# Start of an FNet and gMLP kernel: x's first tiles from three queues, row 0 normed by VectorE, row 3's statistics by ScalarE

## The chip, the cores and the metric

The kernel runs on one core of a Trainium2 chip. The metric is the device time of one execution in microseconds (us). The engines are called TensorE (PE, with its weight loads PEld), VectorE (DVE), ScalarE (ACT), GpSimd (POOL) and SyncE (SP). SP, ScalarE and POOL can each issue DMAs; an instruction waits in the queue of its engine until those ahead of it have gone.

## The reference

All in float32, for one batch of S = 2048 rows and D = 512 columns:

```python
sa, ca, ga, sb, cb, gb = split(silu(c) @ w_mod, 6)
h = layernorm(x) * (1 + ca) + sa
a, b = h @ dft_hid_re.T, h @ dft_hid_im.T
x = x + ga * (dft_seq_re @ a - dft_seq_im @ b)        # FNet
h = layernorm(x) * (1 + cb) + sb
z = gelu(h @ w_in); z1, z2 = z[:, :896], layernorm(z[:, 896:])
x = x + gb * ((z1 * (w_sp @ z2 + b_sp)) @ w_out)      # gMLP
```

## The kernel before

A float32 product is made of three products of float32r parts: each operand is split into a high part (`hi`, by a copy that rounds) and a low part (`lo`, by a subtraction), and `matmul3` adds hi x hi, hi x lo and lo x hi.

The first stage is the product of the sequence matrices with the normed rows of x. It goes in 128 steps of 12 matmuls of 512 columns (`mm_a`). A step n takes one row tile s of x (128 rows) and one slice of a matrix block. For the first 32 steps (the first 512 output columns) blocks of `dft_seq_re` and `dft_seq_im` alternate every four steps, and row tiles 0 to 3 serve steps 0 to 7, tiles 4 to 7 the next eight, and so on. Steps 0 to 3 have an order of their own, line by line of operands: hi x hi for four column blocks, then the two mixed products.

What a step needs is prepared by these pieces:

- `load_x(g, ks, engs)` loads row tiles ks of group g in four DMAs, one for 32 partitions each, and goes through the queues of `engs` in turn. `load_block` loads a matrix block of 512 x 512 in four DMAs (or half of each row of it, s0 to s1); `load(b)` does so for block b into one of two `stage` buffers, by SP.
- `turn_one` and `turn_two` transpose one or two slices of a block on VectorE (lines 173 and 211). `prep_hi(n)` makes the high part `ah` (ScalarE, line 224; for step 0 VectorE, line 222) and `prep_lo(n)` the low part `al` (VectorE, line 230).
- `stats_first(s)` takes mean and variance of row tile s on VectorE (lines 348, 350), adds epsilon (351), takes the power -0.5 on POOL (352) and forms -mean x rstd on POOL (353). `norm_x(s)` norms the tile on ScalarE (line 119) into `xn`. `hi_h(s)` makes its high part `hh` on ScalarE (line 390), `lo_h(s)` its low part `hl` on VectorE (line 395). Column 0 of `xn` is set to 1 by POOL.
- `sum_x(s)` and `square_x(s)` are the other way to the statistics, used for row tiles from 10 on: ScalarE copies the tile and sums it (line 360), POOL scales the sum (361); ScalarE squares and sums (365), and POOL scales, takes the power and multiplies (366 to 368).
- `keep_busy(n, k)` gives TensorE n products of ones (line 311) whose result nobody reads, while the first loads are under way.
- `load_columns(j)` loads a block of `w_mod`; `weigh_column` transposes and weighs a slice of it on VectorE (lines 173 and 295), `sum_column` sums it on ScalarE (line 300), `scale_columns` finishes. `load_ht(j)` loads the hidden matrix into the buffer that the block of `w_mod` with j = 1 had.

The order of work on each engine is the order in which the program writes it (`manual_schedule`). Before step 0 it is written out by hand. From step 0 on, `prep(n)` puts `prep_lo(n + 2)`, the transpose for n + 4, and `prep_hi(n + 3)` ahead of step n, and `run(n)` calls what `at(n, ...)` has put down for that step, after its products. `al` has three buffers and `ah` four, so the preparation can be two to three steps ahead.

Of the kernel before, what the change touches and what calls it, by code (L numbers as in the profile page):

```python
# [8 lines left out]
F32 = mybir.dt.float32  # L9
F32R = mybir.dt.float32r  # L10
AF = mybir.ActivationFunctionType
ALU = mybir.AluOpType

P = 128
# [5 lines left out]
def fnet_gmlp_kernel(  # L20
# [32 lines left out]
    nc = tc.nc  # L53
    S, D = x.shape[1:]
# [11 lines left out]
    def pool(name, side="left", bufs=1):  # L66
        return tc.tile_pool(name=name, bufs=bufs, side=side, reuse_waits="tile")
# [11 lines left out]
    def bank(k, name):  # L79
        return psum.tile([P, 512], F32, tag=f"bank{k}", bufs=1, name=name)  # L80
# [37 lines left out]
    def apply(dst, src, scale_shift):  # L118
        nc.scalar.activation(dst, src, AF.Identity, bias=scale_shift[1], scale=scale_shift[0])
# [3 lines left out]
    def at(n, f, *a):  # L123
        fill.setdefault(n, []).append((f, a))
# [23 lines left out]
    def load_block(tile_, a, s0=0, s1=P, engs=(nc.sync,)):  # L148
        v = a.rearrange("(b j) (a s) -> a j b s", j=32, a=4)
        for q in range(4):  # L150
            engs[q % len(engs)].dma_start(tile_[32 * q:32 * q + 32, :, s0:s1], v[q][:, :, s0:s1])
# [20 lines left out]
    def squares(dst, block, k):  # L172
        nc.vector.transpose(dst.rearrange("p (b i) -> p b i", i=32), block[:, :, 32 * k:32 * k + 32])
# [13 lines left out]
    def slot(n):  # L187
        if n % 2 == 0:
            t = blocks.tile([P, 2, Q], F32, tag="t", bufs=2, name=f"t{n}")
            T[n], T[n + 1] = t[:, 0, :], t[:, 1, :]  # L190
        return T[n]

    def turn_one(n):
        squares(slot(n), stage[n // 4], n % 4)
# [22 lines left out]
    def prep_hi(n, eng=None):  # L217
        if n >= NE:
            return
        AH[n] = blocks.tile([P, Q], F32R, tag="ah", bufs=4, name=f"ah{n}")  # L220
        if eng:
            eng.tensor_scalar(AH[n], T[n], 1.0, None, op0=ALU.mult)
        else:
            nc.scalar.activation(AH[n], T[n], AF.Copy)  # L224

    def prep_lo(n):
        if n >= NE:
            return
        AL[n] = blocks.tile([P, Q], F32R, tag="al", bufs=3, name=f"al{n}")
        nc.vector.tensor_tensor(AL[n], T.pop(n), AH[n].bitcast(F32), op=ALU.subtract)  # L230
# [6 lines left out]
    spool = s1.enter_context(pool("spool", "right"))  # L237
# [5 lines left out]

    ccol = cpool.tile([P, ND], F32, name="ccol")
    ones = cpool.tile([P, P], F32, name="ones")
    nc.gpsimd.memset(ones, 1.0)
    mhalf = cpool.tile([P, 1], F32, name="mhalf")
    nc.gpsimd.memset(mhalf, -0.5)
    sc = cpool.tile([P, ND], F32, name="sc")
    busy = rows.tile([P, D], F32, tag="row", bufs=6, name="busy")  # L250
    nc.vector.memset(busy, 1.0)
# [55 lines left out]
    def keep_busy(n, k):  # L307

        ps = bank(k, "busyp")
        for _ in range(n):  # L310
            nc.tensor.matmul(ps, ones, busy, start=True, stop=True)
# [14 lines left out]
    X, XG, LN, NRM, h_hi, h_lo = {}, {}, {}, {}, {}, {}  # L326

    def load_x(g, ks=range(4), engs=(nc.sync,)):

        if g not in XG:  # L330
            if g % 2:
                XG[g] = spool.tile([P, 4, D], F32, tag="x", bufs=1, name=f"x{g}")
            else:
                XG[g] = hpool.tile([P, 4, D], F32, tag="h12", bufs=1, name=f"x{g}")
        k0, k1 = ks[0], ks[-1] + 1
        v = x.rearrange("(g a k i) d -> g a i k d", g=NQ, a=4, i=32)
        for a in range(4):
            engs[a % len(engs)].dma_start(XG[g][32 * a:32 * a + 32, k0:k1, :], v[g, a][:, k0:k1, :])
        for k in ks:
            X[4 * g + k] = XG[g][:, k, :]  # L340
# [1 line left out]
    def stats_x(s):  # L342
        NRM[s] = norm([X[s]], "x")

    def stats_first(s):

        m = spool.tile([P, 12], F32, tag="first", bufs=4, name=f"first{s}")
        nc.vector.bn_stats(m[:, :6], X[s])
        mv = m[:, 8:]
        nc.vector.bn_aggr(mv[:, :2], m[:, :6])  # L350
        nc.vector.tensor_scalar(mv[:, 1:2], mv[:, 1:2], EPS, None, op0=ALU.add)
        nc.gpsimd.tensor_tensor(mv[:, 2:3], mv[:, 1:2], mhalf, op=ALU.pow)
        nc.gpsimd.tensor_scalar(mv[:, 3:4], mv[:, 0:1], mv[:, 2:3], -1.0, op0=ALU.mult, op1=ALU.mult)
        NRM[s] = mv[:, 2:3], mv[:, 3:4]

    def sum_x(s):

        LN[s] = spool.tile([P, D], F32, tag="xn", bufs=4, name=f"xn{s}")
        m = NRM[s] = spool.tile([P, 4], F32, tag="sums", bufs=3, name=f"sums{s}")
        nc.scalar.activation(LN[s], X[s], AF.Copy, accum_out=m[:, 0:1])  # L360
        nc.gpsimd.tensor_scalar(m[:, 0:1], m[:, 0:1], -1.0 / D, 1.0, op0=ALU.mult, op1=ALU.mult)

    def square_x(s):
        m = NRM[s]
        nc.scalar.activation(LN[s], X[s], AF.Square, bias=m[:, 0:1], accum_out=m[:, 1:2])
        nc.gpsimd.tensor_scalar(m[:, 1:2], m[:, 1:2], 1.0 / D, EPS, op0=ALU.mult, op1=ALU.add)
        nc.gpsimd.tensor_tensor(m[:, 2:3], m[:, 1:2], mhalf, op=ALU.pow)
        nc.gpsimd.tensor_tensor(m[:, 3:4], m[:, 0:1], m[:, 2:3], op=ALU.mult)
        NRM[s] = m[:, 2:3], m[:, 3:4]

    def norm_x(s):

        if s not in LN:
            LN[s] = spool.tile([P, D], F32, tag="xn", bufs=4, name=f"xn{s}")
        if s > 3:
            nc.gpsimd.memset(LN[s][:, 0:1], 1.0)
        apply(LN[s][:, 1:], X.pop(s)[:, 1:], NRM.pop(s))

    def parts_h(s, t):

        return t[s].rearrange("p k (a i) -> p k a i", i=32), LN[s].rearrange("p (a k i) -> p k a i", a=4, i=32)

    def hi_h(s):
        if s < 12:
            h_hi[s] = hpool.tile([P, ND, P], F32R, name=f"hh{s}")
        else:
            if s == 12:
                h_hi["last"] = hpool.tile([P, 4, ND, P], F32R, tag="h12", bufs=1, name="hh12")
            h_hi[s] = h_hi["last"][:, s - 12]
        nc.scalar.activation(*parts_h(s, h_hi), AF.Copy)  # L390

    def lo_h(s):
        h_lo[s] = hpool.tile([P, ND, P], F32R, name=f"hl{s}")
        lo, h = parts_h(s, h_lo)
        nc.vector.tensor_tensor(lo, h, parts_h(s, h_hi)[0].bitcast(F32), op=ALU.subtract)
        LN.pop(s)
# [375 lines left out]


    both = (nc.sync, nc.scalar)
    load_x(0, range(1), both)
    stage[0] = blocks.tile([P, 16, P], F32, tag="stage", bufs=2, name="stage0")
    load_block(stage[0], src[0], 0, P // 2, both)
    load_x(0, range(1, 2), both)
    nc.scalar.activation(sc, ones[:, :ND], AF.Silu)
    load_x(0, range(2, 4))  # L780
    load_block(stage[0], src[0], P // 2, P)
    load(1)
    load_x(1, range(2))
    keep_busy(4, 5)
    for s in range(4):
        LN[s] = spool.tile([P, D], F32, tag="xn", bufs=4, name=f"xn{s}")
        nc.gpsimd.memset(LN[s][:, 0:1], 1.0)
    stats_first(0)
    norm_x(0)
    hi_h(0)  # L790
    turn_one(0)
    prep_hi(0, nc.vector)
    stats_first(1)
    lo_h(0)
    prep_lo(0)
    norm_x(1)
    hi_h(1)
    turn_one(1)
    prep_hi(1)
    stats_first(2)  # L800
    prep_lo(1)
    lo_h(1)
    norm_x(2)
    hi_h(2)
    turn_one(2)
    prep_hi(2)
    stats_first(3)
    turn_one(3)
    prep_hi(3)
    norm_x(3)  # L810
# [7 lines left out]
    at(2, load_row)  # L818
    at(9, silu_row)
    at(4, load_x, 2)  # L820
    at(5, load_columns, 1)
    at(8, load_x, 3)
    at(12, load_columns, 0)
    at(19, load_ht, 0)
    at(28, load_ht, 1)
    for s, n in ((4, 4), (5, 4), (6, 6), (7, 6), (8, 10), (9, 10)):
        m = n + (s == 9)
# [4 lines left out]
    for s, n in zip(range(10, NS), (11, 12, 15, 16, 18, 19)):  # L832
# [2 lines left out]
        at(n + 2, norm_x, s)  # L835
        at(n + 3, hi_h, s)
        at(n + 4, lo_h, s)
    for j, ns in ((1, (12, 14, 17, 18)), (0, (21, 22, 23, 24))):
        for k, n in enumerate(ns):
            at(n, weigh_column, j, k)  # L840
            at(n + 1, sum_column, j, k)
    at(20, scale_columns)

    def change_pools():
        s1.close()
# [225 lines left out]
```

## Time and profile before

| | |
|---|---|
| median of 3 runs | 956.17 us (956.03 to 956.31) |
| profiled execution | 957.03 us |
| its span, first to last instruction | 955.2 us |
| TensorE busy | 948.1 us (99%) |
| VectorE, ScalarE, POOL busy | 674.7, 367.1, 169.0 us |
| granted TensorE clock | 1.000 |

The profile lists for each engine when an instruction started, how long it took, and what ended the idle time before it. A number in the prediction like L395 is the line of the kernel, `hl<-xn,hh` are the tiles written and read, and x4 counts merged instructions.

### The profile page before, as it was taken

How to read it: one execution, taken by the hardware profiler on the slowest of the kernel's cores; microseconds unless marked ns; L12 is line 12 of the kernel's file. 1: busy time of each engine (PE TensorE's matmuls, PEld its weight loads, DVE VectorE, ACT ScalarE, POOL GpSimd, SP SyncE). 2: the span in 40 equal slices, each digit the busy share in tenths (PEclk: the TensorE clock that was granted, in tenths of full speed). 3: DMA queues.
4: the chain of work that ended last, by engine and by line, in shares of the span. 5: the costliest groups of instructions: out<-in, count | busy, mean ns of one | idle time of the engine just before them, and what ended most of it. 6: DMA issues, size and time to landing. Idle time of an engine off the chain costs nothing.

```text
span 955.2 us, 12247 instructions
## 1 busy us (share of the span) xinstructions
PE 948.1 (99%) x4196; PEld 788.1 (83%) x4196; DVE 674.7 (71%) x995; ACT 367.1 (38%) x630; POOL 169.0 (18%) x328
## 2 busy tenths in 40 slices
PE   8999999999999999999999999999999999999998
PEld 5878888888888888888888999888888888888886
DVE  6799857775575757765445577877778688885882
ACT  4585424232232212331444356634544343331221
POOL 2421000221621235114313344200000000000000
PEclk9999999999999999999999999999999999999999
DMA  9997553576538975995499854555545355833541
GB/s 208 218 217 153 116 137 90 148 180 154 143 78 212 276 216 147 273 265 154 154 287 302 308 183 155 145 135 132 138 114 120 90 132 133 209 92 121 192 164 60
DMA packets 249679, 161.27 MB, mean 169 GB/s; under 512 B 130192, under 2 KB 218512, under 8 KB 249488
## 3 DMA queue, kind: packets, MB, share of 16 engines
q1 hardware_dynamic: 236800, 122.59, 53.3%
q0 software_dynamic: 11424, 37.24, 10.6%
q10 hardware_dynamic: 1392, 0.66, 0.3%
q8 instruction: 33, 0.54, 0.3%
q14 instruction: 30, 0.25, 0.1%
HBM read 123.73 MB, written 36.70 MB: 168 GB/s over the span
## 4 chain that ended last, share of the span: by engine, by line
PE 98%; DVE 1%; DMA 0%; ACT 0%; issue 0%; POOL 0%; ACTq 0%; DVEq 0%
PE gp L96 12%; PE gp L97 12%; PE gp L95 12%; PE gw L97 10%; PE gw L95 10%; PE gw L96 9%; PE yp L95 3%; PE yp L97 3%; PE yp L96 3%; PE z2p L95 3%; PE z2p L96 3%; PE z2p L97 3%; PE op L97 3%; PE op L96 3%; PE z1p L97 3%; PE z1p L95 3%
## 5 line engine op out<-in xcount | busy, mean ns | idle before, releaser
L224 ACT ACTIVATE ah<-t 128x512 fp32r<-128x512 f32 x271 | 169.7, 627 | 345.8 <-PE gp L97 183.9
L230 DVE TENSOR_TENSOR al<-t,ah 128x512 fp32r<-128x512 f32 x272 | 185.7, 686 | 165.2 <-PE gp L96 63.7
L96 PE MATMUL gp<-al,hh 128*128 128x512 f32 x496 | 193.1, 389 | 0.6 <-DVE al L230 0.6
L95 PE MATMUL gp<-ah,hh 128*128 128x512 f32 x496 | 193.0, 389 | 0.0
L97 PE MATMUL gp<-ah,hl 128*128 128x512 f32 x496 | 192.9, 389 | 0.0
L97 PE MATMUL gw<-ah,bl 128*128 128x512 f32 x400 | 155.6, 389 | 0.0
L96 PE MATMUL gw<-al,bh 128*128 128x512 f32 x400 | 155.6, 389 | 0.0
L95 PE MATMUL gw<-ah,bh 128*128 128x512 f32 x400 | 155.6, 389 | 0.0
L96 PEld LDWEIGHTS gp<-al,hh 128*128 128x128 f32 x496 | 93.1, 188 | 20.2 <-DVE al L230 1.0
L95 PEld LDWEIGHTS gp<-ah,hh 128*128 128x128 f32 x496 | 93.1, 188 | 19.4
L97 PEld LDWEIGHTS gp<-ah,hl 128*128 128x128 f32 x496 | 93.1, 188 | 19.3
L211 DVE STREAM_TRANSPOSE t<-stage 128x1024 f32<-128x1024 f32 x70 | 86.7, 1239 | 7.8 <-DMA stage<-in_A_dft_seq_re_dram 6.6
L97 PEld LDWEIGHTS gw<-ah,bl 128*128 128x128 f32 x400 | 75.1, 188 | 15.7
L96 PEld LDWEIGHTS gw<-al,bh 128*128 128x128 f32 x400 | 75.1, 188 | 15.7
L95 PEld LDWEIGHTS gw<-ah,bh 128*128 128x128 f32 x400 | 75.1, 188 | 15.4
L205 DVE STREAM_TRANSPOSE t<-stage 128x1024 f32<-128x1024 f32 x56 | 69.4, 1239 | 0.8 <-DMA stage<-in_B_w_sp_dram 0.8
L617 POOL DMA_DIRECT2D s_d<-sj x64 | 35.2, 551 | 125.0 <-DVE sj L609 88.8
L639 ACT ACTIVATE bh<-z 128x512 fp32r<-128x512 f32 (+1 forms) x56 | 32.8, 586 | 61.8 <-PE gw L96 61.8
L95 PE MATMUL yp<-hth,gh 128*128 128x512 f32 x128 | 49.8, 389 | 0.0
L96 PE MATMUL yp<-htl,gh 128*128 128x512 f32 x128 | 49.8, 389 | 0.0
L97 PE MATMUL yp<-hth,gl 128*128 128x512 f32 x128 | 49.8, 389 | 0.0
L96 PE MATMUL z2p<-wil,ah 128*128 128x448 f32 x128 | 46.7, 365 | 0.0
(155 smaller groups left out, 1362.1 us busy)
## 6 DMA issues: line engine op xcount, KB each, us to landing
stage<-in_A_dft_seq_im_dram SPq DMA_DIRECT2D x64, 256.0 KB, 5.4
sj<-in_B_w_sp_dram SPq DMA_DIRECT2D x32, 512.0 KB, 7.7
s_d<-sj POOLq DMA_DIRECT2D x64, 256.0 KB, 4.5
stage<-s_d SPq DMA_DIRECT2D x128, 128.0 KB, 2.9
stage<-in_A_dft_seq_re_dram SPq DMA_DIRECT2D x60, 256.0 KB, 5.3
stage<-in_B_w_sp_dram SPq DMA_DIRECT2D x96, 128.0 KB, 3.0
stage<-h_d SPq DMA_DIRECT2D x32, 256.0 KB, 5.3
z_d<-z POOLq DMA_DIRECT2D x28, 256.0 KB, 6.6
```

Source lines behind the costliest of these rows:

```text
L95: nc.tensor.matmul(acc, ah, bh, start=first, stop=False, skip_group_check=go_on)
L96: nc.tensor.matmul(acc, ah, bl, start=False, stop=False, skip_group_check=go_on)
L97: nc.tensor.matmul(acc, al, bh, start=False, stop=last, skip_group_check=go_on)
L205: nc.vector.transpose(t.rearrange("p r (b i) -> p r b i", i=32), st[:, :, :, 16 * k:16 * k + 32])
L211: nc.vector.transpose(t.rearrange("p k (b i) -> p k b i", i=32), st[:, :, 32 * k:32 * k + 64].rearrange("p b (k i) -> p k b i", k=2))
L224: nc.scalar.activation(AH[n], T[n], AF.Copy)
L230: nc.vector.tensor_tensor(AL[n], T.pop(n), AH[n].bitcast(F32), op=ALU.subtract)
L617: nc.gpsimd.dma_start(s_d[m, r, g][b * P:(b + 1) * P, :], a)
L639: nc.scalar.activation(BH[p, k][:, :w], b_of(p, k), AF.Copy)
```

## The change

Loads: row tile 0 of x goes by SP, ScalarE and twice POOL, tile 1 by SP, POOL, ScalarE and POOL, tiles 2 and 3 by POOL alone. Before, SP and ScalarE shared tiles 0 and 1, and SP loaded tiles 2 and 3. The memset of `ones` moves from POOL to VectorE; POOL's other memsets come after its loads.

Row statistics: tile 0 is normed by VectorE itself (subtract the mean, times rstd). For tiles 1 and 2 VectorE instead of POOL forms -mean x rstd. Tile 3 takes its statistics by `sum_x` and `square_x`; `sum_x(3)` stands right after `hi_h(0)`, `square_x(3)` ahead of `stats_first(2)`. The order of `lo_h`, `prep_lo`, `norm_x` and `hi_h` of the first tiles is changed.

One idle product is left out (3 instead of 4). The load of `w_mod`'s columns 1 moves from step 5 to step 6, behind the load of block 4; their weighing from steps 12, 14, 17, 18 to 15, 17, 18, 20; `scale_columns` from 20 to 22; the load of the first hidden matrix from 19 to 21.

```diff
--- before.py
+++ after.py
@@ -243,9 +243,8 @@
 
     ccol = cpool.tile([P, ND], F32, name="ccol")
     ones = cpool.tile([P, P], F32, name="ones")
-    nc.gpsimd.memset(ones, 1.0)
+    nc.vector.memset(ones, 1.0)
     mhalf = cpool.tile([P, 1], F32, name="mhalf")
-    nc.gpsimd.memset(mhalf, -0.5)
     sc = cpool.tile([P, ND], F32, name="sc")
     busy = rows.tile([P, D], F32, tag="row", bufs=6, name="busy")
     nc.vector.memset(busy, 1.0)
@@ -342,7 +341,7 @@
     def stats_x(s):
         NRM[s] = norm([X[s]], "x")
 
-    def stats_first(s):
+    def stats_first(s, fold=True):
 
         m = spool.tile([P, 12], F32, tag="first", bufs=4, name=f"first{s}")
         nc.vector.bn_stats(m[:, :6], X[s])
@@ -350,8 +349,12 @@
         nc.vector.bn_aggr(mv[:, :2], m[:, :6])
         nc.vector.tensor_scalar(mv[:, 1:2], mv[:, 1:2], EPS, None, op0=ALU.add)
         nc.gpsimd.tensor_tensor(mv[:, 2:3], mv[:, 1:2], mhalf, op=ALU.pow)
-        nc.gpsimd.tensor_scalar(mv[:, 3:4], mv[:, 0:1], mv[:, 2:3], -1.0, op0=ALU.mult, op1=ALU.mult)
         NRM[s] = mv[:, 2:3], mv[:, 3:4]
+        if fold:
+            nc.vector.tensor_scalar(mv[:, 3:4], mv[:, 0:1], mv[:, 2:3], -1.0, op0=ALU.mult, op1=ALU.mult)
+        else:
+            nc.vector.tensor_scalar(LN[s][:, 1:], X.pop(s)[:, 1:], mv[:, 0:1], mv[:, 2:3],
+                                    op0=ALU.subtract, op1=ALU.mult)
 
     def sum_x(s):
 
@@ -372,7 +375,7 @@
 
         if s not in LN:
             LN[s] = spool.tile([P, D], F32, tag="xn", bufs=4, name=f"xn{s}")
-        if s > 3:
+        if s > 2:
             nc.gpsimd.memset(LN[s][:, 0:1], 1.0)
         apply(LN[s][:, 1:], X.pop(s)[:, 1:], NRM.pop(s))
 
@@ -772,39 +775,40 @@
 
 
     both = (nc.sync, nc.scalar)
-    load_x(0, range(1), both)
+    load_x(0, range(1), (nc.sync, nc.scalar, nc.gpsimd, nc.gpsimd))
     stage[0] = blocks.tile([P, 16, P], F32, tag="stage", bufs=2, name="stage0")
     load_block(stage[0], src[0], 0, P // 2, both)
-    load_x(0, range(1, 2), both)
+    load_x(0, range(1, 2), (nc.sync, nc.gpsimd, nc.scalar, nc.gpsimd))
+    load_x(0, range(2, 4), (nc.gpsimd,))
+    for s in range(3):
+        LN[s] = spool.tile([P, D], F32, tag="xn", bufs=4, name=f"xn{s}")
+        nc.gpsimd.memset(LN[s][:, 0:1], 1.0)
+    nc.gpsimd.memset(mhalf, -0.5)
     nc.scalar.activation(sc, ones[:, :ND], AF.Silu)
-    load_x(0, range(2, 4))
     load_block(stage[0], src[0], P // 2, P)
     load(1)
     load_x(1, range(2))
-    keep_busy(4, 5)
-    for s in range(4):
-        LN[s] = spool.tile([P, D], F32, tag="xn", bufs=4, name=f"xn{s}")
-        nc.gpsimd.memset(LN[s][:, 0:1], 1.0)
-    stats_first(0)
-    norm_x(0)
+    keep_busy(3, 5)
+    stats_first(0, False)
     hi_h(0)
+    sum_x(3)
     turn_one(0)
     prep_hi(0, nc.vector)
     stats_first(1)
+    norm_x(1)
+    hi_h(1)
     lo_h(0)
     prep_lo(0)
-    norm_x(1)
-    hi_h(1)
     turn_one(1)
     prep_hi(1)
+    square_x(3)
     stats_first(2)
+    lo_h(1)
     prep_lo(1)
-    lo_h(1)
     norm_x(2)
     hi_h(2)
     turn_one(2)
     prep_hi(2)
-    stats_first(3)
     turn_one(3)
     prep_hi(3)
     norm_x(3)
@@ -818,10 +822,10 @@
     at(2, load_row)
     at(9, silu_row)
     at(4, load_x, 2)
-    at(5, load_columns, 1)
+    at(6, load_columns, 1)
     at(8, load_x, 3)
     at(12, load_columns, 0)
-    at(19, load_ht, 0)
+    at(21, load_ht, 0)
     at(28, load_ht, 1)
     for s, n in ((4, 4), (5, 4), (6, 6), (7, 6), (8, 10), (9, 10)):
         m = n + (s == 9)
@@ -835,11 +839,11 @@
         at(n + 2, norm_x, s)
         at(n + 3, hi_h, s)
         at(n + 4, lo_h, s)
-    for j, ns in ((1, (12, 14, 17, 18)), (0, (21, 22, 23, 24))):
+    for j, ns in ((1, (15, 17, 18, 20)), (0, (21, 22, 23, 24))):
         for k, n in enumerate(ns):
             at(n, weigh_column, j, k)
             at(n + 1, sum_column, j, k)
-    at(20, scale_columns)
+    at(22, scale_columns)
 
     def change_pools():
         s1.close()
```

## The prediction

> **What bounds the kernel now.** I read the page first, then busy time by stage, then TensorE's waits, then the timeline of the first 22 us. Stage rows: stretch, its length, then busy us (instructions) of PE, PEld, DVE, ACT, POOL, granted clock, DMA share, GB/s.
>
> ```profile
> span 955.2 us, 12247 instructions
> PE 948.1 (99%) x4196; PEld 788.1 (83%) x4196; DVE 674.7 (71%) x995; ACT 367.1 (38%) x630; POOL 169.0 (18%) x328
> ...
> 0.00:8.00 8.00, 6.47 (x9) 2.60 (x9) 2.87 (x7) 2.93 (x4) 1.40 (x12) 1.00 0.71 183
> 8.00:21.20 13.20, 11.73 (x48) 8.53 (x48) 12.00 (x23) 7.17 (x11) 4.69 (x6) 1.00 1.08 220
> ...
> 40.00:60.00 20.00, 19.45 (x86) 15.77 (x85) 12.96 (x20) 14.16 (x32) 6.96 (x23) 1.00 1.16 218
> 60.00:80.00 20.00, 20.00 (x90) 16.57 (x89) 19.76 (x31) 16.52 (x38) 5.29 (x17) 1.00 1.13 214
> ...
> PE gp L415 <- ACT ah L224: 1.1, 2, 0.7
> PE gp L96 <- DVE al L230: 0.6, 1, 0.6
> ```
>
> TensorE is the bound: 99% busy, and after the start its only listed wait is one of 0.6 us. The edits all lie in the first 85 us, so they can change the time in two places: when TensorE's products become continuous, and that one stall. At the start VectorE is the bound (12.00 of 13.20 us busy); from 8 us the DMA engines are full too.
>
> In the rows below (start us, duration, engine, line, operation) a product step is 12 matmuls; steps 0 to 3 are those of L415.
>
> ```profile
> 3.79 0.69 DVE L348 BATCH_NORM_STATS2 first<-x 128x6 f32<-128x512 f32 x1 [2.41 <-DMA x<-in_A_x_dram]
> ...
> 5.05 0.56 POOL L352 TENSOR_TENSOR first<-first,mhalf 128x1 f32<-128x1 f32 x1 [3.95 <-DVE first L351]
> ...
> 6.61 0.71 DVE L173 STREAM_TRANSPOSE t<-stage 128x512 f32<-128x512 f32 x1 [1.72 <-DMA stage<-in_A_dft_seq_re_dram]
> ...
> 7.93 1.17 PE L415 MATMUL gp<-ah,hh 128*128 128x512 f32 x4
> ...
> 8.64 0.15 DVE L351 TENSOR_SCALAR first<-first 128x1 f32<-128x1 f32 x1
> 8.72 0.69 DVE L395 TENSOR_TENSOR hl<-xn,hh 128x512 fp32r<-128x512 f32 x1
> ...
> 9.33 0.68 DVE L230 TENSOR_TENSOR al<-t,ah 128x512 fp32r<-128x512 f32 x1
> ...
> 9.93 0.70 DVE L173 STREAM_TRANSPOSE t<-stage 128x512 f32<-128x512 f32 x1
> ...
> 10.56 0.65 DVE L348 BATCH_NORM_STATS2 first<-x 128x6 f32<-128x512 f32 x1
> ...
> 11.46 0.15 DVE L351 TENSOR_SCALAR first<-first 128x1 f32<-128x1 f32 x1
> 11.61 0.61 ACT L224 ACTIVATE ah<-t 128x512 fp32r<-128x512 f32 x1
> 11.70 0.55 POOL L352 TENSOR_TENSOR first<-first,mhalf 128x1 f32<-128x1 f32 x1 [1.51 <-DVE first L351]
> ...
> 12.26 0.69 DVE L230 TENSOR_TENSOR al<-t,ah 128x512 fp32r<-128x512 f32 x1 [0.64 <-ACT ah L224]
> ...
> 12.35 1.25 POOL L353 TENSOR_SCALAR first<-first 128x1 f32<-128x1 f32 x1
> ...
> 13.63 0.82 ACT L119 ACTIVATE xn<-x,first 128x511 f32<-128x511 f32 x1 [1.41 <-POOL first L353]
> ```
>
> ```profile
> 15.68 1.19 PE L415 MATMUL gp<-ah,hh 128*128 128x512 f32 x4 [0.39 <-ACT ah L224]
> ```
>
> Step 0 starts at 7.93, step 2 at 15.68, and from there TensorE is nearly continuous. So 15.68 is the number to compare: what step 2 loses or gains, the end loses or gains. Row 2's chain sets it: statistics 10.56, power on POOL 11.70, fold on POOL 12.35 (1.25 us beside VectorE's work), norm 13.63.
>
> **The change part by part.** *The three queues.* POOL gets eight loads, two of row 0, two of row 1, and rows 2 and 3; SP loses six and ScalarE two. POOL's memsets go behind the loads.
>
> ```profile
> 143.12 1.07 POOL L491 DMA_DIRECT2D xr<-in_A_x_dram  x2 [25.59 <-PE qp L471]
> ...
> xr<-in_A_x_dram POOLq DMA_DIRECT2D x2, 256.0 KB, 3.0
> ...
> x<-in_A_x_dram SPq DMA_DIRECT2D x4, 128.0 KB, 2.6
> ...
> x<-in_A_x_dram SPq DMA_DIRECT2D x2, 64.0 KB, 2.1
> ```
>
> The last number of the issue rows is us from issue to landing. Two issues on POOL take 1.07 us, so eight keep it busy for 4.3 us, from about 0.7 to 5.0. Row 0's power, at 5.05 before, is then barely late (up to 0.3). Row 0's last quarter is issued about 1.25 and, at 2.1 to 3.0 us to land, is there between 3.4 and 4.3, against 3.79 now. The first stage's loads leave one issue earlier, but share the DMA engines with POOL's loads (71% busy before 8 us), so they gain little or lose up to 0.7. Row 0's norm on VectorE stands ahead of the transpose of 6.61 and replaces ScalarE's norm (0.8) and POOL's fold; from a power at 5.05 to 5.4 and about half a us of VectorE it ends at 6.2 to 6.6, so the transpose stays near 6.61. I take 0, with -0.3 and +0.7 as ends. One idle product less and the ones set by VectorE cost nothing: TensorE waits for row 0 anyway.
>
> A rule weighed against this: the Trainium skill, "DMA: Bandwidth & Descriptors", section "Issuing engines are not separate DMA queues", says that loads from SP, ScalarE and POOL run on the same 16 engines and interleave, so more issuers save only issue time. By it rows 2 and 3 come no sooner and push the stage's blocks back; taken fully, the sum below would be 0.7 higher. The share of 1.08 from 8 us on agrees that the engines fill.
>
> *Folds on VectorE (rows 1 and 2).* VectorE now waits in its own queue for POOL's power. Row 1: its epsilon ends at 8.64 + 0.15 = 8.79; the power follows 0.09 later and the fold 0.65 after that (11.70 to 12.35), so the fold ends at 8.79 + 0.09 + 0.65 + 0.15 = 9.68. Behind it stand hl, al and the second transpose. Before, hl started at 8.72, the transpose 1.21 later; now it starts at 9.70 + 1.21 = 10.9 and ends at 11.63 (10.63 before). Cost so far 1.0.
>
> *Row 3's statistics on ScalarE.* They take 1.05 us off VectorE (as row 2's, from 10.56 to 11.46 + 0.15) but stand ahead of row 2's power in POOL's queue. A later row shows that path:
>
> ```profile
> 45.37 0.71 ACT L365 ACTIVATE xn<-x,sums 128x512 f32<-128x512 f32 x1
> 45.98 0.19 ACT L365 ACTIVATION_READ_ACCUMULATOR xn<-x,sums 128x1 f32 x1
> ```
>
> ```profile
> 46.26 0.19 POOL L366 TENSOR_SCALAR sums<-sums 128x1 f32<-128x1 f32 x1 [1.98 <-ACT xn L365]
> 46.53 0.55 POOL L367 TENSOR_TENSOR sums<-sums,mhalf 128x1 f32<-128x1 f32 x1
> 47.16 0.20 POOL L368 TENSOR_TENSOR sums<-sums 128x1 f32<-128x1 f32 x1
> ```
>
> From the square's start to the end of POOL's third operation are 47.36 - 45.37 = 1.99 us. In the new order ScalarE does ah of step 1 (starts at 11.66 after the transpose, 0.61), then the square, from 12.27; POOL is free at 14.26; only then row 2's power, and its fold on VectorE ends at 14.26 + 0.08 + 0.65 + 0.15 = 15.1. VectorE has reached that fold at about 12.7 and stands for 2.3 us; hl and al of step 1 are queued behind it. al ends 0.61 + 0.68 later, at 16.4 (12.95 before). TensorE, which has done step 1's first four products from about 12.3, stands for nearly 3 us, then does eight at 0.23: step 2 starts at 18.25. Its hh and ah, by the same durations, are ready at about 17.6, and from step 2 on every operand keeps ahead. **Loss 18.25 - 15.68 = 2.57.**
>
> *Rows 2 and 3 of x from POOL.* ScalarE's sum of row 3 stands in its queue ahead of row 1's norm, and POOL's scaling of it ahead of row 1's power. With 0.9 for the sum (the square's 0.71 + 0.19), 0.2 for the scaling and 0.1 between, the load must land by 7.65 to cost nothing. It is issued last at 4.45 and lands 2.6 to 3.0 us later at best, at 7.1 to 7.5. But the second half of the first stage, 512 KB, now leaves SP in the same time, and at 220 GB/s is worth up to 2.3 us. Ends 0 and 2.1; I take a quarter of that half ahead of it, 0.6.
>
> *w_mod's columns a block later.*
>
> ```profile
> 30.41 6.00 SPq L151 DMA_DIRECT2D wb<-in_w_mod_dram  x4
> 36.51 6.46 SPq L151 DMA_DIRECT2D stage<-in_A_dft_seq_re_dram  x4
> ```
>
> ```profile
> 49.06 1.25 DVE L211 STREAM_TRANSPOSE t<-stage 128x1024 f32<-128x1024 f32 x1 [5.14 <-DMA stage<-in_A_dft_seq_re_dram]
> ...
> 58.97 1.25 DVE L211 STREAM_TRANSPOSE t<-stage 128x1024 f32<-128x1024 f32 x1 [0.65 <-DMA stage<-in_A_dft_seq_im_dram]
> ```
>
> ```profile
> 51.35 0.39 PE L95 MATMUL gp<-ah,hh 128*128 128x512 f32 x1
> 52.29 0.50 PE L96 MATMUL gp<-al,hh 128*128 128x512 f32 x1 [0.55 <-DVE al L230]
> ```
>
> The stage block behind the columns lands about 4.6 us later than it could (1 MB at 220 GB/s); the transpose waits for it, al stands behind the transpose, and TensorE loses 52.29 - 51.35 - 0.23 = 0.71. With the order turned this goes: **gain 0.71**. Next late is the block transposed at 58.97: same bytes ahead of it, so it does not come sooner; it would stall a TensorE that ran over about 1.4 us earlier than without the stall, but here TensorE runs later. The weighing moves by one to three steps into the stretch 60 to 80 us, where VectorE is 99% busy; its cover is the lead of al over the products, and a later TensorE widens it. The lead gone, one weighing would cost about 1.4. The hidden matrix's load waits for the columns' buffer, two steps later, and is hidden by the four steps to its use. Both 0.
>
> **Sum.** +2.57 + 0.6 - 0.71 = +2.5. The profiled execution took 957.03 (span 955.2 and 1.8 around it), 0.86 above the median of 956.17; it would become 959.5, the median 958.6. A change under 0.2% (1.9 us) is one that a measurement of this kernel can hardly tell.
>
> **The rivals.**
> *Row 3 lands late*: POOL's loads wait behind the whole second half, +2.1 instead of 0.6: +4.0, 960.1. For it: the full DMA engines. Against: POOL's loads are issued early. Chance 0.15.
> *The clock falls in step 1's gap.* The granted clock is 1.00 in every stretch, though TensorE paused up to 0.7 us; a pause of 3 us has no row. If the products after it ran at half pace for 15 matmuls, that would add 15 x 0.23 = 3.4 at most, half of it hidden by operands: +4.2, 960.4. The Trainium skill, "TensorE: Matmul & The Clock Gate", Part 1, lets the clock fall after a whole idle window of about 3.4 us; by it the pause is just too short. Chance 0.05.
> *Row 2's power is not held up*: the square and POOL's three operations overlap VectorE's statistics. Then row 2's fold ends at about 13.5, step 2 starts at 16.7, +1.0 + 0.2 - 0.7: +0.5, 956.7. Against it: ah precedes the square on ScalarE, and the square precedes the power on POOL. Chance 0.2.
> *The relief of VectorE wins* (the other side): without POOL's slow folds (1.25 for row 2) and row 3's statistics, al of step 1 comes by 11.3 and TensorE runs on from step 0; step 2 would start at 7.9 + 5.4 = 13.3, of which the block at 58.97 leaves 1.4 plus what the DMAs gain: about -2.0, 954.2. It decides if al is there 1.6 us earlier than now; VectorE's waits for POOL speak against it. Chance 0.08.
>
> **How the numbers follow.** The forecast, loss of 1.2 to 3.3, has 0.5; what is left (0.02) is spread. Its own range is 957.4 to 959.5. Slower than 1.9 us: four fifths of 0.5, with the first two rivals, plus half the rest: 0.6. Faster 0.08, same 0.32. The range leaves out the faster rival and the far ends: 956.0 to 960.4.
>
> **What would show it.** Right: VectorE idle some 2 us ahead of a fold, ended by POOL; POOL's power of row 2 behind ScalarE's square; TensorE idle nearly 3 us between the first and second four products of step 1; step 2 near 18 us; no wait of L96 near 52 us. Wrong: row 3's sum on ScalarE idle for its load beyond 8 us (more loss), the transpose of 6.61 ended by its DMA past 7.3, or the fold of row 2 ended before 14 us (less).

## The result, and the profile after

The changed kernel takes 961.73 us (median of 6 runs, 961.56 to 962.43); the kernel before, run beside it, 956.15 us (956.03 to 956.67). The profiled execution took 961.8 us, with a span of 960.0. The ratio is 1.0059, with a 95% interval of 1.0046 to 1.0072. The change is slower, as forecast, but by 5.6 us where 2.5 were forecast, and the time lies above the predicted range.

The page of the changed kernel:

```profile
span 960.0 us, 12253 instructions
PE 949.4 (99%) x4194; PEld 789.8 (82%) x4194; DVE 674.1 (70%) x996; ACT 368.6 (38%) x633; POOL 169.8 (18%) x334
```

Its second stage (columns as before: stretch, length, busy us of PE, PEld, DVE, ACT and POOL, granted clock, DMA share, GB/s):

```profile
8.00:21.20 13.20, 9.09 (x23) 6.25 (x24) 8.39 (x19) 6.53 (x12) 2.54 (x8) 0.61 0.88 163
```

TensorE's waits (what, for what; us in total, times, longest):

```profile
PE gp L418 <- DVE ah L222: 3.5, 1, 3.5
PE gp L418 <- DVE hl L398: 1.7, 1, 1.7
```

TensorE is busy for 949.4 us in all (948.1 before), so most of the loss is waiting, and all of it lies ahead of step 2. VectorE is busy for 8.39 of the 13.20 us where it was for 12.00: it is no longer what the start waits for, it waits itself. TensorE waits 3.5 us for its first operand and 1.7 us for the first `hl`. The granted clock of 0.61 is a mean; in rows of 2 us it goes down to 0.50 and no lower. So TensorE ran at half speed for (1 - 0.61) x 13.20 / 0.5 = 10.3 us. No row of the kernel before has that.

The timeline of the changed kernel (start us, duration, engine, line, operation; in brackets the idle time before it and what ended it). The lines have moved by some: L415 is now L418, POOL's power L351, the fold on VectorE L354. L350 at 10.87 is row 1's epsilon, and step 4 begins with the first L95.

```profile
1.25 4.33 POOL L337 DMA_DIRECT2D x<-in_A_x_dram  x8 [0.82 <-POOLq L1061]
...
6.54 0.69 DVE L347 BATCH_NORM_STATS2 first<-x 128x6 f32<-128x512 f32 x1 [5.00 <-DMA x<-in_A_x_dram]
...
8.86 0.70 DVE L173 STREAM_TRANSPOSE t<-stage 128x512 f32<-128x512 f32 x1
...
10.16 2.04 PE L418 MATMUL gp<-ah,hh 128*128 128x512 f32 x4 [3.50 <-DVE ah L222]
...
10.87 0.15 DVE L350 TENSOR_SCALAR first<-first 128x1 f32<-128x1 f32 x1
...
11.50 0.63 ACT L363 ACTIVATE xn<-x 128x512 f32<-128x512 f32 x1 [1.89 <-DMA x<-in_A_x_dram]
...
12.31 0.18 POOL L364 TENSOR_SCALAR sums<-sums 128x1 f32<-128x1 f32 x1 [3.96 <-ACT xn L363]
12.47 0.54 POOL L351 TENSOR_TENSOR first<-first,mhalf 128x1 f32<-128x1 f32 x1
13.04 0.21 DVE L354 TENSOR_SCALAR first<-first 128x1 f32<-128x1 f32 x1 [2.02 <-POOL first L351]
...
14.38 0.70 DVE L173 STREAM_TRANSPOSE t<-stage 128x512 f32<-128x512 f32 x1
...
15.65 0.71 ACT L368 ACTIVATE xn<-x,sums 128x512 f32<-128x512 f32 x1
...
17.44 0.20 POOL L371 TENSOR_TENSOR sums<-sums 128x1 f32<-128x1 f32 x1
17.49 1.91 PE L418 MATMUL gp<-ah,hh 128*128 128x512 f32 x4
17.59 0.55 POOL L351 TENSOR_TENSOR first<-first,mhalf 128x1 f32<-128x1 f32 x1
...
18.17 0.22 DVE L354 TENSOR_SCALAR first<-first 128x1 f32<-128x1 f32 x1 [2.11 <-POOL xn L379]
...
19.64 1.24 PE L418 MATMUL gp<-al,hh 128*128 128x512 f32 x4 [0.25 <-DVE al L230]
...
21.64 1.07 PE L418 MATMUL gp<-ah,hh 128*128 128x512 f32 x4
...
27.08 0.39 PE L95 MATMUL gp<-ah,hh 128*128 128x512 f32 x1
```

Three delays are to be seen. Row 0's statistics start at 6.54 (3.79 before); a load of x ended the wait for them. ScalarE stands until 11.50 for row 3's load; POOL's scaling of that sum (12.31) stands ahead of row 1's power (12.47), and the power ahead of the fold (13.04) for which VectorE waited 2.02 us. Then the square of row 3 (15.65) and POOL's three operations (the last at 17.44) stand ahead of row 2's power (17.59), whose fold VectorE reaches 2.11 us too early. Step 2 starts at 21.64 where it started at 15.68.

The DMA issues of the first 8 us, of the changed kernel (columns: tiles, queue, count, KB each, median us from issue to landing):

```profile
stage<-in_A_dft_seq_re_dram SPq DMA_DIRECT2D x6, 128.0 KB, 5.3
x<-in_A_x_dram POOLq DMA_DIRECT2D x4, 128.0 KB, 5.6
...
x<-in_A_x_dram POOLq DMA_DIRECT2D x4, 64.0 KB, 4.6
x<-in_A_x_dram SPq DMA_DIRECT2D x2, 64.0 KB, 3.5
x<-in_A_x_dram ACTq DMA_DIRECT2D x2, 64.0 KB, 3.8
```

and of the kernel before, where those of 128 KB on SP took the 2.6 us shown in the prediction:

```profile
x<-in_A_x_dram SPq DMA_DIRECT2D x4, 64.0 KB, 2.9
x<-in_A_x_dram ACTq DMA_DIRECT2D x4, 64.0 KB, 3.1
```

The four loads of 128 KB, which each hold a quarter of rows 2 and 3, take 5.6 us to land instead of 2.6, and the loads of x in the other queues take longer too. By the trace's queues, POOL's moved 0.57 MB between 6 and 10 us while SP's, by then mostly matrix blocks, moved 0.40 MB beside it, at a DMA share of 1.14 to 1.20. With all loads in SP's queue (the second experiment) rows 2 and 3 go ahead of the second half of the first stage.

### The profile page after: what moved, and what is told of

Same layout as the page of the kernel before. It is cut to its first block, busy times and chain, and to the rows that moved or that the text cites. A ratio compares the mean times of both kernels' runs of the same rounds, so it can differ in the third digit from the quotient of the medians.

```text
span 960.0 us, 12253 instructions
## 1 busy us (share of the span) xinstructions
PE 949.4 (99%) x4194; PEld 789.8 (82%) x4194; DVE 674.1 (70%) x996; ACT 368.6 (38%) x633; POOL 169.8 (18%) x334
## 4 chain that ended last, share of the span: by engine, by line
PE 98%; DMA 1%; SPq 1%; DVE 0%; ACTq 0%; issue 0%; ACT 0%
PE gp L97 12%; PE gp L96 12%; PE gp L95 12%; PE gw L95 9%; PE gw L96 9%; PE gw L97 9%; PE yp L96 3%; PE yp L95 3%; PE yp L97 3%; PE z2p L96 3%; PE z2p L97 3%; PE z2p L95 3%; PE op L97 3%; PE op L95 3%; PE z1p L96 3%; PE z1p L95 3%
## 5 line engine op out<-in xcount | busy, mean ns | idle before, releaser
L95 PE MATMUL gp<-ah,hh 128*128 128x512 f32 x496 | 192.9, 389 | 0.0
L95 PE MATMUL gw<-ah,bh 128*128 128x512 f32 x400 | 155.6, 389 | 0.0
L95 PEld LDWEIGHTS gp<-ah,hh 128*128 128x128 f32 x496 | 93.1, 188 | 19.3
L95 PEld LDWEIGHTS gw<-ah,bh 128*128 128x128 f32 x400 | 75.1, 188 | 15.7
L95 PE MATMUL yp<-hth,gh 128*128 128x512 f32 x128 | 49.8, 389 | 0.0
```

The source lines that it names most:

```text
L95: nc.tensor.matmul(acc, ah, bh, start=first, stop=False, skip_group_check=go_on)
```

## The experiments

Theory A, after the result: row 3's late landing and the queue order set step 2. Rivals: row 0's late landing (B), TensorE at half clock (C). Most kernels undo one part of the change, or do one alone.

**Row 0 from two queues again.**

```diff
-    load_x(0, range(1), (nc.sync, nc.scalar, nc.gpsimd, nc.gpsimd))
+    load_x(0, range(1), both)
```

> The changed kernel, with row tile 0 of x loaded by SP and ScalarE again (rows 1 to 3 stay as changed). Theory 'row 0 is late': row 0 lands near 3.6 us instead of 6.5, everything behind it moves up by 2.2, the granted clock stays at 1, about 959.5. Rival 'row 3 is late': row 1's power is held by row 3's load through POOL's queue, which still lands near 10.5 to 11 us, so row 1's fold stays near 12.5 and the time falls by 0.5 at most, about 961.2, although step 0 starts 2 us earlier.

960.92 us; 1.0048 times before (1.0035 to 1.0061). Row 0's statistics start at 3.77, and step 0 at 8.60 instead of 10.16, but only 0.8 us of that reaches the median. Its timeline, ScalarE's sum of row 3 and step 2:

```profile
10.21 0.63 ACT L363 ACTIVATE xn<-x 128x512 f32<-128x512 f32 x1 [3.37 <-DMA x<-in_A_x_dram]
...
20.30 1.07 PE L418 MATMUL gp<-ah,hh 128*128 128x512 f32 x4
```

ScalarE still stands for row 3. The sum came 1.29 us earlier than in the changed kernel, where POOL had two more loads to issue, and step 2 came 1.34 us earlier.

**All loads as before.**

```diff
-    load_x(0, range(1), (nc.sync, nc.scalar, nc.gpsimd, nc.gpsimd))
+    load_x(0, range(1), both)
...
-    load_x(0, range(1, 2), (nc.sync, nc.gpsimd, nc.scalar, nc.gpsimd))
-    load_x(0, range(2, 4), (nc.gpsimd,))
+    load_x(0, range(1, 2), both)
+    load_x(0, range(2, 4))
```

> The changed kernel with all of x's first loads through SP and ScalarE as before; the new order of the operations stays. Row 3 then lands near 9.4 us, row 1's fold on VectorE ends near 11.3, and step 2 starts 8.25 after that, near 19.6 instead of 21.4: about 959.8, still 3.6 over the kernel before. If the loads were the whole loss it would be about 955.5 (the stall at 52 us gone).

959.61 us; 1.0036 (1.0022 to 1.0050). The three queues are worth 2.1 us of the loss. The same rows, and SP's issues:

```profile
2.82 4.26 SPq L337 DMA_DIRECT2D x<-in_A_x_dram  x6
...
9.41 0.63 ACT L363 ACTIVATE xn<-x 128x512 f32<-128x512 f32 x1 [2.61 <-DMA x<-in_A_x_dram]
...
19.51 1.08 PE L418 MATMUL gp<-ah,hh 128*128 128x512 f32 x4
```

Row 3, issued last by SP, is there 2.09 us earlier than from POOL, and step 2 is 2.13 us earlier. But ScalarE waits for it here too, 2.61 us.

**The columns a block later, alone** (on the kernel before).

```diff
-    at(5, load_columns, 1)
+    at(6, load_columns, 1)
...
-    at(19, load_ht, 0)
+    at(21, load_ht, 0)
...
-    for j, ns in ((1, (12, 14, 17, 18)), (0, (21, 22, 23, 24))):
+    for j, ns in ((1, (15, 17, 18, 20)), (0, (21, 22, 23, 24))):
...
-    at(20, scale_columns)
+    at(22, scale_columns)
```

> The kernel before with only w_mod's columns, their weighing and the hidden matrix's load moved. The stall of 0.71 near 52 us goes: about 955.4. Rival 'the stall only moves': the DMA engines are full, a later transpose waits instead, and the time stays at 956.1.

956.07 us; 0.9998 (0.9989 to 1.0006): no difference to be seen. A gain of 0.71 us would be 0.9993 and lies inside this interval, so this run alone does not rule it out; the second profile of the kernel before, below, says more.

**Five idle products instead of three** (against theory C: TensorE is given work until step 0).

```diff
-    keep_busy(3, 5)
+    keep_busy(5, 5)
```

> The changed kernel with five idle products instead of three, which keep TensorE busy until about 10 us, where step 0 starts. Theory 'the half clock is hidden': the granted clock stays at 1 throughout, the first products are faster, but step 1's mixed products wait for VectorE's al at 19.6 all the same: 0.2 less, about 961.5. Rival 'the half clock is the loss': steps 0 and 1 take about 4 us less and the end moves with them, about 958.

961.75 us; 1.0057 (1.0045 to 1.0070). The mean granted clock is 0.996 in all five executions (0.994 to 0.996 in those of the changed kernel), and the time stays the same. The clock was expected to stay at 1 and did not: it still fell in the pause after step 0's first products, so this run tests theory C only in part.

**The square of row 3 behind row 2's statistics** (with the loads as before).

```diff
-    square_x(3)
     stats_first(2)
+    square_x(3)
```

> The kernel of the run with loads as before (959.6), with row 3's square moved behind row 2's statistics, so that row 2's power is ahead of the square's three operations in POOL's queue. Theory 'POOL's queue held row 2': VectorE's fold of row 2 ends at 14.9 instead of 16.3 and step 1's al at 16.1 instead of 17.5. TensorE at half clock is then the next to be late: step 1's first four products run to 17.0, so step 2 starts near 18.85 instead of 19.5: about 959.0. If the queue did not matter: 959.6.

958.29 us; 1.0024 (1.0014 to 1.0034): 1.3 us less than with the square in front. Its timeline, from row 2's fold to the mixed products of step 1:

```profile
14.81 0.21 DVE L354 TENSOR_SCALAR first<-first 128x1 f32<-128x1 f32 x1 [0.66 <-POOL first L351]
...
15.54 0.69 DVE L230 TENSOR_TENSOR al<-t,ah 128x512 fp32r<-128x512 f32 x1
15.58 1.91 PE L418 MATMUL gp<-ah,hh 128*128 128x512 f32 x4
...
17.29 1.25 PE L418 MATMUL gp<-al,hh 128*128 128x512 f32 x4
```

The fold waits 0.66 us for POOL where it waited 2.11. The operand `al` is done at 16.23 and TensorE takes it up only at 17.29, without idling: its first four products of step 1 took 1.71 us at half clock. Here theory C shows: in this execution 1.1 us.

**The same with idle products in the gap.**

```diff
+                if n == 0 and b is ah and a is h_hi[s]:
+                    keep_busy(1, 5)
```

> The run before this one, with one idle product put between the first four and the other eight products of step 0, where TensorE stands for 2.9 us. Theory 'the half clock is late next': the granted clock stays at 1, step 0 is done at 13.7, step 1 waits only for al (16.1), step 2 starts near 18.0: 0.85 less than without it, about 958.1. Rival 'the clock is still hidden': no difference.

958.39 us; 1.0022 (1.0014 to 1.0031): not better than without them. In its profile step 2 starts at 17.97 instead of 19.28, but the two profiles differ more than the medians do: the profiled execution of the kernel without idle products was one of its longest, 959.44 us. The executions by their mean clock say more. With the idle product, those at 1.000 took 958.13 to 958.70 us, those at 0.997 or 0.998 958.12 to 958.70: the half clock of these costs nothing that shows. Without it, the five at 0.998 took 958.07 to 958.29 us and the four at 0.996 or 0.994 958.83 to 959.71: there it costs about 1 us, which the median does not show.

**The sum of row 3 behind row 1's norm** as well (still with the loads as before).

```diff
-    sum_x(3)
     turn_one(0)
...
     norm_x(1)
     hi_h(1)
+    sum_x(3)
```

> Loads as before, square behind row 2's statistics, and row 3's sum on ScalarE moved behind row 1's norm and high part, so that row 1's power does not wait for row 3's load. Theory 'row 3 stands ahead of rows 1 and 2 in POOL's and ScalarE's queues, and that is the whole loss beside the loads': row 1's fold ends at 9.4 instead of 11.2, row 2's at 13.2, step 1's al at 14.5, step 2 starts at 16.4 to 16.6, the clock stays at 1: about 956.8. Rival 'VectorE's folds and the norm of row 0 on VectorE cost by themselves': it stays above 958.

956.65 us; 1.0003 (0.9995 to 1.0012): the loss is gone, but for what the interval hides. Its timeline, the folds of rows 1 and 2, step 2 and step 4:

```profile
9.49 0.21 DVE L354 TENSOR_SCALAR first<-first 128x1 f32<-128x1 f32 x1 [0.67 <-POOL first L351]
...
13.18 0.21 DVE L354 TENSOR_SCALAR first<-first 128x1 f32<-128x1 f32 x1 [0.67 <-POOL first L351]
...
16.61 1.08 PE L418 MATMUL gp<-ah,hh 128*128 128x512 f32 x4
...
22.05 0.39 PE L95 MATMUL gp<-ah,hh 128*128 128x512 f32 x1
```

Each fold waits only 0.67 us, for the power of its own row. The granted clock is 1.000 again in this execution. Row 3's statistics on ScalarE and the folds on VectorE cost little by themselves: step 2 is 1.04 us later than in the second profile of the kernel before (15.57, below), step 4 0.73 later (22.05 against 21.32), and the median 0.4, within the noise. What stood ahead of what made the loss. No run has this order together with the three queues.

**The three queues alone** (on the kernel before, old order of work).

```diff
-    load_x(0, range(1), both)
+    load_x(0, range(1), (nc.sync, nc.scalar, nc.gpsimd, nc.gpsimd))
...
-    load_x(0, range(1, 2), both)
+    load_x(0, range(1, 2), (nc.sync, nc.gpsimd, nc.scalar, nc.gpsimd))
+    load_x(0, range(2, 4), (nc.gpsimd,))
...
-    load_x(0, range(2, 4))
```

POOL's memsets stand behind its loads and `ones` is set by VectorE, as in the change.

> The kernel before with only the loads of x's first tiles through three queues (POOL's memsets behind its loads, ones set by VectorE); the order of operations is the old one. Row 0 then lands near 6.5 instead of 3.6, its statistics run ahead of the first transpose, row 0's high part comes near 10.2 and its low part 1.5 later than before; row 3's late landing (near 11) is hidden, because its statistics start at 14: about 957.8. If the late row 0 went through at its full 2.9: 959.2. If the loads cost only in the new order: 956.3.

957.82 us; 1.0017 (1.0009 to 1.0026). Nobody asks for row 3 early here, and the loads still cost 1.6 us:

```profile
6.81 0.69 DVE L347 BATCH_NORM_STATS2 first<-x 128x6 f32<-128x512 f32 x1 [5.28 <-DMA x<-in_A_x_dram]
...
10.80 2.07 PE L414 MATMUL gp<-ah,hh 128*128 128x512 f32 x4 [2.68 <-ACT hh L389]
...
23.35 0.39 PE L95 MATMUL gp<-ah,hh 128*128 128x512 f32 x1
```

That is row 0's lateness, theory B: its statistics are 3.0 us late. Of these, 2.0 are left at step 4 (23.35 against 21.32 in the second profile of the kernel before, shown below), and 1.6 in the median. TensorE ran at half the clock for part of this stretch too (the last section), but that is the smaller part: the one execution with a mean clock of 1.000 took 957.64 us, those at 0.998 957.58 to 958.09.

**The columns a block later, and two folds on VectorE where it waits anyway** (on the kernel before): the fold of row 2 behind its statistics, that of row 3 behind `turn_one(3)`, rows 0 and 1 on POOL.

```diff
-        nc.gpsimd.tensor_scalar(mv[:, 3:4], mv[:, 0:1], mv[:, 2:3], -1.0, op0=ALU.mult, op1=ALU.mult)
+        FOLD[s] = lambda eng: eng.tensor_scalar(mv[:, 3:4], mv[:, 0:1], mv[:, 2:3], -1.0, op0=ALU.mult, op1=ALU.mult)
+        if s < 3:
+            FOLD[s](nc.gpsimd if s < 2 else nc.vector)
...
+    FOLD[3](nc.vector)
```

> The kernel before with w_mod's columns a block later and the folds of rows 2 and 3 on VectorE at places where it waits anyway (row 2's right behind its statistics, row 3's behind the fourth transpose); loads, row 0, row 1 and row 3's statistics as before. If what the changed kernel took from POOL is worth something once nothing stands ahead of it, row 2's norm starts at 12.4 instead of 13.4, step 2 at 15.1 instead of 15.45, and step 3 no longer waits for its high part: 0.65 less than the columns alone, about 955.4. Rival: VectorE's wait for POOL's power costs what the fold gains, 956.1.

956.15 us; 1.0000 (0.9990 to 1.0009). Step 2 starts earlier, and waits in its second line:

```profile
14.82 1.11 PE L419 MATMUL gp<-ah,hh 128*128 128x512 f32 x4
...
16.53 1.20 PE L419 MATMUL gp<-al,hh 128*128 128x512 f32 x4 [0.59 <-DVE al L230]
```

The hoped-for 955.4 would be within the interval, but the trace speaks against it. What step 2 gains is lost again at `al`: step 3 starts at 18.48, against 18.46 in the second profile of the kernel before. In the old order VectorE's own work is the bound of the start (12.28 of 13.20 us busy here), and a fold moved over from POOL takes nothing off it.

**The kernel before once more**, unchanged, profiled again: was the stall at 52 us part of the kernel?

> The kernel before, unchanged, once more with a profile. If the stall of 0.7 near 52 us belongs to every execution, it is in this trace and the span is near 955.2. If it belonged to the one execution that was profiled (0.9 over the median), the trace has none or a smaller one and the span is near 954.4.

956.10 us; 0.9999 (0.9989 to 1.0010). Its timeline, step 2, step 4 and the block that had been transposed at 49.06:

```profile
15.57 1.20 PE L415 MATMUL gp<-ah,hh 128*128 128x512 f32 x4 [0.39 <-ACT ah L224]
...
21.32 0.39 PE L95 MATMUL gp<-ah,hh 128*128 128x512 f32 x1
...
47.62 1.25 DVE L211 STREAM_TRANSPOSE t<-stage 128x1024 f32<-128x1024 f32 x1 [3.80 <-DMA stage<-in_A_dft_seq_re_dram]
```

and its stage from 40 to 60 us:

```profile
40.00:60.00 20.00, 20.00 (x90) 16.57 (x89) 14.23 (x23) 15.68 (x35) 7.37 (x24) 1.00 1.20 223
```

The block came 1.4 us earlier and TensorE is busy for all 20.00 us (19.45 in the first profile). The span is 954.3 us instead of 955.2. The stall belonged to the one execution that was profiled first.

**The first stage's loads behind x** (on the changed kernel; its first half by SP alone).

```diff
-    stage[0] = blocks.tile([P, 16, P], F32, tag="stage", bufs=2, name="stage0")
-    load_block(stage[0], src[0], 0, P // 2, both)
...
     load_x(0, range(2, 4), (nc.gpsimd,))
+    stage[0] = blocks.tile([P, 16, P], F32, tag="stage", bufs=2, name="stage0")
+    load_block(stage[0], src[0], 0, P // 2)
```

> The changed kernel with the first half of the stage block issued by SP alone and behind row tiles 0 and 1, so that until about 4 us POOL's loads of row 0 share the DMA engines with x alone. If sharing with the stage's loads made POOL's quarters late, they land by 3.9 and the statistics of row 0 start near 4. If POOL's own path is late, the statistics still start at 5 or later. The stage block comes later here, so the time says nothing: it may be 1 to 2 over the changed kernel.

961.75 us (one run). POOL's four loads of 64 KB, two of row 0 and two of row 1, now take 3.3 us to land (the median) instead of 4.6; those of rows 2 and 3 take 6.0, where they took 5.6 (DMA issues, then timeline):

```profile
x<-in_A_x_dram POOLq DMA_DIRECT2D x4, 128.0 KB, 6.0
x<-in_A_x_dram POOLq DMA_DIRECT2D x4, 64.0 KB, 3.3
```

```profile
4.67 0.69 DVE L347 BATCH_NORM_STATS2 first<-x 128x6 f32<-128x512 f32 x1 [3.14 <-DMA x<-in_A_x_dram]
...
11.50 0.63 ACT L363 ACTIVATE xn<-x 128x512 f32<-128x512 f32 x1 [3.77 <-DMA x<-in_A_x_dram]
```

Row 0's statistics come 1.87 us earlier than in the changed kernel, row 3's sum at the same 11.50, and step 2 at 21.58 instead of 21.64. So, by this one run, the 2.75 us by which row 0 was late are, for the larger part, the price of sharing the DMA engines with the stage's loads (1.87), for the rest (0.88) what is left with the stage's loads out of the way, POOL's later issue among it. But the stage's block is now late itself (its transpose moves only from 8.86 to 8.62), and both lie under row 3's wait. For rows 2 and 3 this run does not part sharing from a slower path of POOL's own: the stage's loads, which SP issues from 1.64 to 7.22 us here, are still in flight with them.

**Idle products all through** (the changed kernel with five ahead of step 0 and the idle product in the gap), to take the half clock out.

> The changed kernel with five idle products ahead of step 0 and one more between the first four and the other eight products of step 0 (five ahead alone did not keep the clock up). Theory 'the half clock is hidden in the changed kernel': with the clock at 1, or at half for one window at most, step 1's first four products end some 2 us earlier and then wait for VectorE's al at 19.6: 961.5, within 0.3 of the changed kernel. Rival 'the half clock is part of the loss': 960.5 or less.

963.36 us (962.05 to 963.8); 1.0073 (1.0059 to 1.0087): slower by 1.6 us, at a mean clock of 0.998. Neither forecast came true. Row 3 landed later still (its sum starts at 12.13), and TensorE's wait for `al` is this:

```profile
20.27 1.20 PE L418 MATMUL gp<-al,hh 128*128 128x512 f32 x4 [1.10 <-DVE al L230]
```

With less time at half clock TensorE waits 1.10 us for `al` instead of 0.25: a faster TensorE only idles longer. Why the load came 0.6 us later, and what the last us of the median is, was not settled.

Six kernels have row 3's sum and square in the order of the change, with five landings between them:

| kernel | row 3's sum starts | step 2 starts | between |
|---|---|---|---|
| loads as before | 9.41 | 19.51 | 10.10 |
| row 0 from two queues | 10.21 | 20.30 | 10.09 |
| five idle products | 11.29 | 21.54 | 10.25 |
| the change | 11.50 | 21.64 | 10.14 |
| stage behind x | 11.50 | 21.58 | 10.08 |
| idle products all through | 12.13 | 22.23 | 10.10 |

Whatever row 0, the stage's block and the clock did, step 2 followed 10.1 us (10.25 once) behind the start of row 3's sum, whose wait a load of x ended each time. That decides for theory A.

## Why the prediction was right in sign and wrong in size

**The queue order: right.** It named VectorE idle for 2.3 us ahead of row 2's fold behind ScalarE's square and POOL's three operations; 2.11 were measured. From the end of step 1's transpose to step 2 it had 18.25 - 11.63 = 6.62 us; measured were 21.64 - 15.08 = 6.56. The closeness is in part luck: `al` was done 0.26 us sooner after the transpose than reckoned, and TensorE took 0.2 us longer from there. Moving the square gave 1.3 us back, moving the sum 1.6 more.

**Row 3's landing: the step that failed.** The prediction took 0.6 us, with 2.1 as the far end. By its own working, step 2 with row 3 in time starts at 18.25; it started at 21.64, so the term is 3.4. The late landing was a rival with a chance of 0.15: it did occur, and its price of 2.1 was too low as well. Its mechanism is borne out in part: POOL's loads shared the engines with SP's blocks between 6 and 10 us (0.57 and 0.40 MB), they did not wait until all of these had gone. The 10.1 us put the time by which row 3 was needed at 18.25 - 10.1 = 8.15. With the loads of the kernel before it is there at 9.41, which is 1.3 us too late: that part belongs to asking for row 3 early. From POOL it is there at 11.50: the other 2.1 are the three queues'. These 2.1 have a second claimant: row 1's epsilon ended at 10.87 + 0.15 = 11.02, since row 0 was late, so with row 3 in time its fold would have started 0.67 us after that, at about 11.7 instead of 13.04. By this estimate only about 1.3 of the 3.4 us are row 3's alone. The error lay in carrying 2.6 us to land, a row of the kernel before, over to a kernel in which POOL's eight loads are in flight together with those of the other two queues; the same size took 5.6. How much of this is sharing and how much a slower path of POOL's own, no run separates. The prediction weighed the Trainium skill's "Issuing engines are not separate DMA queues" ("DMA: Bandwidth & Descriptors") at 0.7 us. The rows agree with that section: issue ended 1.5 us sooner (1.25 + 4.33 = 5.58 on POOL, 2.82 + 4.26 = 7.08 on SP) and that was all that was saved, for the data came 2.1 us later.

**Row 0: taken at 0, up to 0.7; measured 2.25 at the first transpose** (8.86 for 6.61). Two causes: POOL's first load left at 1.25 instead of 0.7, and POOL's loads of 64 KB took 4.6 us to land where 2.1 to 3.0 were reckoned. So this term failed too. In the changed kernel it is hidden under row 3, as the table shows; in the old order the three queues cost 1.6 us.

**The stall: taken as a gain of 0.71; it is 0.** The prediction read it from the only execution it had, which was 0.86 us above the median, and went on to subtract both. The columns alone moved nothing clear of the noise, and the second profile of the kernel before has no stall. Its absence after the change, foreseen as a sign that the step was right, proved nothing.

**The clock fell, which had a chance of 0.05**, but not where it was looked for: it was at half from before step 0's first product at 10.16, and not from a gap in step 1, for 10.3 us instead of some 3.4. On the path it weighs next to nothing. TensorE ended step 1's first four products 0.25 us before `al` came. The pause of nearly 3 us foreseen within step 1 did not appear, since the halved clock filled it.

**The sum again:** 2.57 + 3.4 + 0 = 6.0 at step 2 (21.64 - 15.68 = 5.96); it fits because the 3.4 were taken from it. That what step 2 loses the end loses was not quite right: from step 2 to step 4 the kernel before takes 5.75 us and the changed one 5.44, so some 0.3 us are regained there. Against the kernel before without the stall, the shift at step 4 is 27.08 - 21.32 = 5.76, the spans differ by 960.0 - 954.3 = 5.7, and the medians by 5.6. Nothing to speak of was lost or regained behind step 4.

## What to carry to other kernels

When a step is moved to an engine with slack, ask what its input's landing time is and who stands behind it in that in-order queue: row 3's statistics took load off VectorE, but a sum that waits for the last load of the start held up the power of a row that had long been there. Loads spread over more queues were issued 1.5 us sooner here and landed 2.1 us later, beside full DMA engines; do not price a landing by a row that was taken with other loads in flight. A stall seen in one profiled execution that is longer than the median is no part of the kernel until a second profile shows it.

## What was not expected of the hardware

The granted clock fell to half after pauses shorter than the 3.4 us for which it then stayed there. With the three queues alone TensorE paused 2.68 us; its rows of 2 us each:

```profile
10.00:12.00 2.00, 1.20 (x3) 1.01 (x4) 1.26 (x3) 1.06 (x3) 1.32 (x2) 0.69 1.24 214
12.00:14.00 2.00, 2.00 (x7) 1.52 (x6) 1.93 (x6) 1.62 (x3) 0.14 (x1) 0.50 1.25 218
14.00:16.00 2.00, 2.00 (x10) 1.68 (x9) 2.00 (x4) 0.82 (x1) 1.04 (x2) 0.96 1.23 218
```

(0.31 x 2 + 0.50 x 2 + 0.04 x 2) / 0.5 = 3.4 us at half. In the kernel with the idle product in the gap a pause of 2.07 us, behind one of 1.17 us, was enough. Pauses of 1.43 and 1.58 us, in the profiled execution of the kernel with the sum behind row 1, left it at 1.00. The Trainium skill, "TensorE: Matmul & The Clock Gate", Part 1, has it fall after at least one idle window of about 3.4 us. The length of the stretch agrees with that window, but a pause shorter than it was enough here. How often it falls differs from execution to execution of one kernel: in that with the square behind row 2, executions with a mean clock of 0.998 took 958.07 to 958.29 us, those with 0.996 or 0.994 958.83 to 959.71.
